# Block summaries of an attention kernel: sums of v by TensorE, maxima of k in token layout, query copies in a row, and a new order of steps

## Chip, core and metric

The program runs on one core of one Trainium2 chip. The metric is device time in microseconds (us) of one launch, on the slowest (here the only) core. Engines: TensorE (PE; PEld is its weight load), VectorE (DVE), ScalarE (ACT), GpSimd (POOL), SyncE (SP). Loads of q and k are issued by POOL (the software queue q0, which turns f32 into f16 on the way), all other transfers by SP (the hardware queue q1); 16 DMA engines serve both.

## The reference, cut to what matters

```python
# first part: q, k, v of shape (4, 8, 768, 64); blocks of 32 tokens, window 16
k_sum = k.reshape(B, H, nb, block, D).max(axis=3)       # 24 block maxima of k per head
v_sum = v.reshape(B, H, nb, block, D).mean(axis=3)      # 24 block means of v per head
scores_l = scale * q @ k.T                              # kept where |i - j| < 16
scores_s = scale * q @ k_sum.T + log(block)
a = softmax(concat[scores_l masked, scores_s])
x = a @ concat[v, v_sum]                                # heads side by side: (4, 768, 512)
# second part: 4 experts (Hd = 64), the best 2 of 4 by x @ w_gate with softmax weights w
for e in range(4):
    y = softmax_causal(scale * (x @ wq[e]) @ (x @ wk[e]).T) @ (x @ wv[e]) @ wo[e]
    out += w[e] * y
```

## The kernel before

There are four batches b. **Stage 1** is the first part of the reference, for a pair c of two heads at a time (c = 0 to 3, two pairs to a group g of four heads). A window of 96 keys and the 24 block maxima (120 rows) meet 64 queries in one score product; there are 12 such windows per head. The steps of a pair, in the names of the plan: `dk`, `dq` load k and q of a group as f16; `tk`, `tq` transpose them on TensorE; `ck`, `cq` copy the transposes from PSUM to kT and qT; `rk` takes the block maxima of kT (L305); `kw` and `ksc` put the windows and the maxima into kw; `sc` makes scores in two halves (mask by L361, product by L368), `ex` the exponentials aT, `av` the product with vb in f32 (L385, two halves), `rc` and `xm` divide, `tx` transposes back (L410), `hi` and `lo` split x into two f16 parts.

vb holds for each window its 96 rows of v and below them, in rows 96 to 119, the 24 block sums of the head, repeated for all 12 windows. The rows of v come by `dv` from memory (96 x 24 pieces of 256 B for a pair). The sums come in three steps: `dvs` loads v of a group a second time, with a block's 32 tokens side by side in one partition (tile vs, 768 KB); `tr` adds halves to halves, five additions on VectorE or POOL (L247); `ds` writes the result into vb by two transfers on SP's queue, which repeat each row 12 times (72 KB each).

**Stage 2** is the second part, for a batch: `pp` projects to queries and keys (L558), `vp` to values and gate logits (L493, L496), `ga` to `gc` compute the gate, `sp` scores (L582), `es` exponentials (L590), `dm` the causal mask on the diagonal (POOL, L595), `aw` the weighted values (L606), `r2`, `wv` weights them, `tw`, `ct` transposes, `op` projects out (L647), `oc` copies and `od` stores. The weights are loaded and cast once (`dw`, `dwv`, `dwo`, `cw`, `cvg`, `co`).

The order of all 734 steps, the engine of each, and the buffer that it takes are written in a table (L50 to L104); the program issues them as they stand there, and an engine and its queue keep that order. SLOTS gives the number of buffers of each kind. The qT copy `cq` writes, in even batches, with a step between elements, and in odd ones in a row:

```python
if b % 2:
    copy(e, dst.rearrange("c (p s) -> c p s", s=6), src.rearrange("c (s p) -> c p s", s=6))
else:
    copy(e, dst.rearrange("c (p s) -> c s p", s=6), src.rearrange("c (s p) -> c s p", s=6))
```

Of the kernel before, what the change touches and what calls it, by code (L numbers as in the profile page):

```python
# [50 lines left out]
19,S,0 4,G, 5,V, 20,V, 17,G,0 88,P,0.0 6,G, 21,V, 8,G, 22,V, 68,P,1.1 0,G,1 18,G,0 89,V, 91,A,0 73,P,0.0 3,G,1  # L51
69,V, 70,V,0 71,A,1 93,P,1.1 1,G, 72,A, 90,V,1 48,P,2.0 74,A, 94,A, 7,G, 77,P,4.0 78,A, 92,V, 23,G, 24,G,
95,P,0.1 75,P,6.2 76,A, 49,V, 51,V,2 50,V,1 52,V, 67,S,0 25,G,1 97,P,2.3 98,A, 66,S, 80,P,4.0.0 2,G, 53,P,6.2
54,V, 79,P, 28,P,2.1 9,S,1 81,V, 15,G, 96,A, 82,V, 33,P,3.0 29,V, 83,P,0.0.0 84,A, 57,P,4.4 58,A, 31,V,1
55,P,6.5 56,A, 213,G,2 283,P,2.0 30,V,0 32,A, 284,A, 87,S,2 86,S, 99,P,4.1.1 34,V, 35,P,2.0 36,A, 214,G,2
288,P,6.1 205,G,0 26,S, 10,G, 11,G, 85,V, 289,A, 37,P,0.2 12,G, 13,G, 14,G, 286,V,0 27,S, 100,P, 285,V,1
287,V, 101,V, 102,V, 223,P,2.1 224,V, 243,P,3.0 268,P,6.2 269,V, 292,P,4.1 38,A, 226,A,2 103,P,0.1.1 104,A,
244,V, 245,V,0 633,G,3 225,V,1 293,A, 227,V, 290,P,6.3 40,P,2.0.0 291,A, 105,V, 206,G,0 247,A,1 248,P,4.0
# [721 lines left out]
```

## Time and profile before

| what | us |
|---|---|
| median of 3 runs (lowest, highest) | 207.64 (206.0, 210.47) |
| the profiled execution's own time | 208.41 |
| its span on the chip | 206.4 |
| TensorE busy | 149.7 |
| VectorE busy | 131.6 |
| ScalarE busy | 123.1 |
| GpSimd busy | 82.8 |

The span runs from the first to the last recorded event of that execution; its own time is what was measured around it. Busy time is the sum in which an engine had an instruction at work; matmuls are pipelined, so a busy TensorE need not be at its peak. The DMA queues moved 33.17 MB in 65499 packets, 54208 of them under 512 B. A wait is put down to the event that ended it; `issue` is a wait for which the profile shows nothing.

### The profile page before, as it was taken

The page shows a single profiled execution, that of the slowest core. Times are in us where ns is not written, and L with a number is a line of the kernel's source. Part 1 is how long each engine was busy: PE and PEld are TensorE (multiplying, and loading weights), DVE is VectorE, ACT ScalarE, POOL GpSimd, SP SyncE. Part 2 cuts the span into 40 slices and gives each one's busy share as a digit, 9 for nine tenths or more (in the row PEclk, how much of TensorE's full clock was granted, in tenths as well). Part 3 has the DMA queues.
Part 4 walks back from the last instruction along what each step waited for, and adds up shares of the span by engine and source line. Part 5 has one row for each costly group of instructions (what it writes and reads, how often), then busy time and mean ns, then how long its engine had stood idle before and what let it go on. Part 6 is the DMA issues. An engine that isn't in the chain of part 4 may idle for free.

```text
span 206.4 us, 6279 instructions
## 1 busy us (share of the span) xinstructions
PE 149.7 (73%) x2704; PEld 115.2 (56%) x2704; DVE 131.6 (64%) x227; ACT 123.1 (60%) x152; POOL 82.8 (40%) x146
## 2 busy tenths in 40 slices
PE   0252277897369974737977978766999999999960
PEld 0242175686356753637754567655768767767620
DVE  0653029987666467604839998967498687636940
ACT  2199402658265854517997777344646888698740
POOL 7980009304520634236553954918722012223300
PEclk9999999999969999988999999999699999999997
DMA  6999999699999999999167997999698580200456
GB/s 154 187 150 187 223 175 148 80 183 208 167 199 230 168 163 183 204 210 246 24 105 128 219 184 113 219 260 265 105 175 166 139 137 17 89 3 0 165 194 254
DMA packets 65499, 33.17 MB, mean 161 GB/s; under 512 B 54208, under 2 KB 61376, under 8 KB 64704
## 3 DMA queue, kind: packets, MB, share of 16 engines
q1 hardware_dynamic: 58016, 26.48, 67.4%
q0 software_dynamic: 7456, 6.29, 20.2%
q8 instruction: 21, 0.34, 0.7%
q14 instruction: 6, 0.05, 0.1%
HBM read 30.41 MB, written 6.29 MB: 178 GB/s over the span
## 4 chain that ended last, share of the span: by engine, by line
PE 41%; DVE 21%; DMA 17%; issue 10%; ACT 6%; SPq 1%; POOL 1%; DVEq 0%; POOLq 0%; ACTq 0%
PE ps L385 9%; PE ps L558 7%; DMA vb<-in_v_dram 7%; DMA vb<-vs 7%; DVE qT L163 4%; PE ps L410 4%; PE ps L493 4%; PE ps L647 4%; PE ps L582 3%; DMA kn<-in_k_dram 3%; DVE ks L305 3%; PE ps L334 2%; PE ps L606 2%; PE ps L296 2%; DVE x L400 2%
## 5 line engine op out<-in xcount | busy, mean ns | idle before, releaser
L590 ACT ACTIVATE a<-ps 128x1024 f16<-128x1024 f32 (+1 forms) x48 | 42.0, 915 | 14.1 <-PE ps L582 12.6
L385 PE MATMUL ps<-vb,aT 120*64 120x65 f32 x768 | 30.1, 241 | 14.7 <-DMA vb<-in_v_dram 7.1
L595 POOL TENSOR_SCALAR_AFFINE_SELECT a<-a 128x256 f16<-128x256 f16 x48 | 18.9, 410 | 54.4 <-ACT a L590 49.6
L247 POOL TENSOR_TENSOR vs<-vs 96x1024 f32<-96x1024 f32 (+4 forms) x23 | 25.3, 1100 | 31.4 <-DMA vs<-in_v_dram 20.7
L385 PEld LDWEIGHTS ps<-vb,aT 120*64 120x64 f32 x768 | 27.8, 154 | 17.5 <-issue 11.9
L375 ACT ACTIVATE aT<-ps 120x768 f32<-120x768 f32 x32 | 25.2, 819 | 14.2 <-PE ps L368 11.3
L558 PE MATMUL ps<-hi,wqk 128*128 128x384 f16 x128 | 22.6, 326 | 1.6 <-ACT aT L375 1.6
L163 DVE COPY qT<-ps 128x768 f16<-128x768 f16 x6 | 12.9, 2145 | 12.4 <-PE ps L334 12.2
L163 POOL COPY kw<-kT 128x960 f16<-128x960 f16 (+1 forms) x14 | 15.7, 1153 | 11.6 <-PE ps L368 8.1
L410 PE MATMUL ps<-id,x 128*128 128x128 f32 x96 | 16.8, 320 | 4.5 <-issue 1.6
L421 DVE TENSOR_TENSOR lo<-ps,hi 128x768 f16<-128x768 f32 x16 | 15.4, 971 | 5.2 <-ACT hi L161 5.0
L361 PE MATMUL ps<-pi,mt 64*128 64x64 f16 (+1 forms) x128 | 12.8, 271 | 7.0 <-issue 3.3
L558 PEld LDWEIGHTS <-wqk 128*128 128x128 f16 x128 | 12.1, 98 | 9.4 <-issue 1.9
L296 PE MATMUL ps<-id,kn 96*64 96x96 f16 x256 | 10.1, 244 | 9.1 <-DMA kn<-in_k_dram 8.7
L410 PEld LDWEIGHTS ps<-id,x 128*128 128x128 f32 x96 | 12.7, 162 | 6.6 <-issue 2.1
L247 DVE TENSOR_TENSOR vs<-vs 96x512 f32<-96x512 f32 (+4 forms) x17 | 10.5, 615 | 8.9 <-DMA vs<-in_v_dram 7.0
L582 PE MATMUL ps<-qk,qk 64*128 64x512 f16 (+3 forms) x128 | 14.6, 307 | 2.1 <-DVE x L400 1.2
L368 PE MATMUL ps<-qT,kw 64*128 64x64 f16 x384 | 12.8, 204 | 4.2 <-ACT qT L161 2.3
L400 DVE TENSOR_TENSOR x<-ps,rec 128x768 f32<-128x768 f32 x16 | 15.3, 957 | 0.6
L161 ACT COPY qT<-ps 128x768 f16<-128x768 f16 x10 | 15.6, 1612 | 0.1
L161 ACT CAST hi<-ps 128x768 f16<-128x768 f32 x9 | 7.4, 825 | 13.5 <-PE ps L410 13.4
L305 DVE TENSOR_REDUCE ks<-kT 128x24 f16<-128x768 f16 x16 | 14.9, 944 | 0.1
(81 smaller groups left out, 260.8 us busy)
## 6 DMA issues: line engine op xcount, KB each, us to landing
vb<-in_v_dram SPq DMA_DIRECT2D x14, 576.0 KB
vs<-in_v_dram SPq DMA_DIRECT2D x8, 768.0 KB
out_dram<-ob SPq DMA_DIRECT2D x12, 512.0 KB
kn<-in_k_dram POOLq DMA_DIRECT2D x7, 384.0 KB, 6.9
qn<-in_q_dram POOLq DMA_DIRECT2D x7, 384.0 KB, 7.6
vb<-vs SPq DMA_DIRECT2D x32, 72.0 KB
vb<-in_v_dram SPq DMA_DIRECT2D x2, 552.0 KB
a<-in_moe_wq_dram SPq DMA_DIRECT2D x4, 128.0 KB
```

The costliest lines, as they stand in the source:

```text
L161: nc.scalar.copy(dst, src)
L163: en(e).tensor_copy(dst, src)
L247: en(e).tensor_tensor(w[:, 0:half], w[:, 0:half], w[:, half:2 * half], AL.add)
L305: nc.vector.tensor_reduce(T["ks"][ks.slot], T["kT"][kT.slot].rearrange("c (s n p) -> c n s p", s=8, n=NSUM), AX.XY, AL.max)
L375: nc.scalar.activation(T["aT"][aT.slot][0:KR], pbank(sc, 2)[0:KR, :, 0:384], AF.Exp, scale=SCALE)
L385: nc.tensor.matmul(pbank(av, 2)[o:o + 64, u, 65 * (2 * (t // 2) + hp):65 * (2 * (t // 2) + hp) + 65], a[0:KR, hp, 64 * t:64 * t + 64], T[" ...
L400: nc.vector.tensor_tensor(T["x32"][x32.slot].rearrange("p (u t w) -> p u t w", u=2, w=64), avv()[:, :, :, 0:64], T["rec"][rec.slot].to_bro ...
L410: nc.tensor.transpose(pbank(xp, 2)[:, t // 3, 128 * (t % 3):128 * (t % 3) + 128], T["x32"][x32.slot][:, 128 * t:128 * t + 128], T["id32"])
L558: nc.tensor.matmul(pbank(pp, 2)[:, u, 0:384], T["wqk"][:, ch, cc, j, :], hi_(ch)[:, 384 * u:384 * u + 384], start=(ch == 0), stop=(ch == N ...
L582: nc.tensor.matmul(pbank(sp, 2)[:, ep, c0:c0 + w], T["qk"][qk[1].slot][r, 128 * tj:128 * tj + 128], T["qk"][qk[0].slot][r, n0:n0 + w], sta ...
L590: nc.scalar.activation(a2v(u), pbank(sp, 2)[:, :, 0:ln], AF.Exp, scale=SCALE / (XS * XS))
L595: nc.gpsimd.affine_select(m, m, [[0, 2], [1, 128]], AL.is_ge, 0.0, base=0, channel_multiplier=-1)
```

## The change

Four things, and a new table.

- Block sums of v: `dvs`, `tr` and the transfers of `ds` go. TensorE sums the 96-row windows that `dv` has loaded: 12 products per head with a slice of a 0/1 matrix `sel` (made once on POOL) accumulate into 24 rows of PSUM (`bs`, L294, f32, 32 weight columns). Four heads lie in four groups of 32 PSUM partitions in batches 1 to 3, two in batch 0. `be` copies the sums to vs, partitions 96 to 119; `ds` is now a copy on POOL, VectorE or ScalarE that repeats them into vb.
- Maxima of k: `km` takes, on the loaded k (token layout, 8 tokens of a partition side by side), maxima of halves in three steps; two more transposes in `tk` bring the result to PSUM, and `rk` reduces only 4 to 1 there.
- q is loaded as 96 x 512 like k, and `cq` always writes qT in a row (its source in PSUM is read with a step).
- The weights are declared in parts (two halves of wqk, values, output), so that a projection waits only for its own.
- The table is new: the steps stand in another order, on partly other engines. vb has six buffers and ks three. The constants in braces in the step calls are the planner's estimates; they do not enter the program.

Core of the diff:

```diff
-SLOTS = dict(qn=3, kn=3, kT=2, ks=2, kw=3, qT=3, aT=6, x32=2, vb=4, vs=2,
+SLOTS = dict(qn=3, kn=3, km=3, kT=2, ks=3, kw=3, qT=3, aT=6, x32=2, vb=6, vs=2,
...
-19,S,0 4,G, 5,V, 20,V, 17,G,0 88,P,0.0 6,G, 21,V, 8,G, 22,V, 68,P,1.1 0,G,1 18,G,0 89,V, 91,A,0 73,P,0.0 3,G,1
+116,S,0 27,G,0 28,G,0 29,V,0 30,V, 31,V, 10,G, 76,P,0.0.0 12,V, 5,G,1 77,A, 94,P,1.1.1 99,P,2.0 78,V, 80,V,0
...
+    def sels(e):
+        z = T["sel"]
+        en(e).memset(z, 0.0)
+        nc.gpsimd.memset(z[:, 22:24], 1.0)
+        nc.gpsimd.affine_select(z[:, 22:24], z[:, 22:24], [[-32, 2]], AL.is_ge, 0.0,
+                                base=-16, channel_multiplier=1)
+        nc.gpsimd.affine_select(z[:, 22:24], z[:, 22:24], [[32, 2]], AL.is_ge, 0.0,
+                                base=47, channel_multiplier=-1)
...
+            for w in (256, 128, 64):
+                def mx(e, w=w, i=i):
+                    hs = slice(n * i, n * i + n)
+                    m = T["km"][km[b, g].slot][:, hs, :]
+                    x = T["kn"][kn[b, g].slot][:, hs, :] if w == 256 else m
+                    en(e).tensor_tensor(m[:, :, 0:w], x[:, :, 0:w], x[:, :, w:2 * w], AL.max)
...
-            nc.sync.dma_start(out=T["vs"][t.slot],
-                              in_=v[b, 4 * g:4 * g + 4].rearrange("h (n s) d -> (h n) (s d)", s=32))
-        R.step(f"dvs{b}{g}", {"S": 0.45}, [], [t], go, dma=2.2)
-        half = 1024
-        while half >= 64:
-            def add(e, half=half):
-                w = T["vs"][t.slot]
-                en(e).tensor_tensor(w[:, 0:half], w[:, 0:half], w[:, half:2 * half], AL.add)
...
-            for hp in range(2):
-                r0 = NSUM * (hh + hp)
-                nc.sync.dma_start(out=w[WIN:KR, 12 * hp:12 * hp + 12, 0:64],
-                                  in_=s[r0:r0 + NSUM, 0:64].unsqueeze(1).to_broadcast((NSUM, NQ, 64)))
...
+    def sums(b, cs):
+        sp, t = R.buf("ps"), R.buf("vs")
+
+        def mm(e):
+            n = 2 * len(cs)
+            for tt in range(NQ):
+                for j in range(n):
+                    nc.tensor.matmul(pbank(sp)[32 * j:32 * j + 32, 0, 0:64],
+                                     T["sel"][:, 22 - 2 * tt:54 - 2 * tt],
+                                     T["vb"][vb[b, cs[j // 2]].slot][0:WIN, 12 * (j % 2) + tt, 0:64],
+                                     start=(tt == 0), stop=(tt == NQ - 1))
...
+        def ev(e):
+            for j in range(2 * len(cs)):
+                copy(e, T["vs"][t.slot][96:120, j, :], pbank(sp)[32 * j:32 * j + NSUM, 0, 0:64])
...
+            def dsum(e, i=i, c=c):
+                copy(e, T["vb"][vb[b, c].slot][WIN:KR, :, 0:64].rearrange("n (h t) d -> n h t d", h=2),
+                     T["vs"][t.slot][WIN:KR, 2 * i:2 * i + 2, :].unsqueeze(2).to_broadcast(
+                         (NSUM, 2, NQ, 64)))
...
+            for hp in range(2):
+                nc.tensor.transpose(pbank16(kp)[64 * hp:64 * hp + 64, 768:864],
+                                    T["km"][km[b, g].slot][:, hh + hp, 0:64], T["id16"][0:96, 0:96])
...
-                                    T["kT"][kT.slot].rearrange("c (s n p) -> c n s p", s=8, n=NSUM),
-                                    AX.XY, AL.max)
+                                    pbank16(kp)[:, 768:864].rearrange("c (n p) -> c n p", p=4),
+                                    AX.X, AL.max)
...
-            if b % 2:
-                copy(e, dst.rearrange("c (p s) -> c p s", s=6),
-                     src.rearrange("c (s p) -> c p s", s=6))
-            else:
-                copy(e, dst.rearrange("c (p s) -> c s p", s=6),
-                     src.rearrange("c (s p) -> c s p", s=6))
+            copy(e, T["qT"][qT.slot].rearrange("c (p s) -> c p s", s=8),
+                 pbank16(qp)[:, 0:S].rearrange("c (s p) -> c p s", s=8))
...
+            for c in (2 * g, 2 * g + 1):
+                load_v(b, c)
+                if b == 0:
+                    sums(b, [c])
+            if b:
+                sums(b, [2 * g, 2 * g + 1])
```

What the new table does to the order, at three places. First SyncE's queue at the start of the program, before (vs are the tiles of the tree, vb those of the products; the number behind a name tells buffers apart):

```order
L240 DMA vs_100<-in_v_dram 96x2048
L286 DMA vb_96<-vs_100 24x12x64 x2
L268 DMA vb_96<-in_v_dram 96x24x64
L240 DMA vs_101<-in_v_dram 96x2048
L286 DMA vb_98<-vs_100 24x12x64 x2
L268 DMA vb_98<-in_v_dram 96x24x64
L262 DMA vb_97<-in_v_dram 80x64
L268 DMA vb_97<-in_v_dram 96x23x64
```

and after (L466, L472 and L459 are loads of weights into buffers named a and wg):

```order
L466 DMA a_136<-in_moe_wq_dram 128x4x64
L275 DMA vb_101<-in_v_dram 80x64
L281 DMA vb_101<-in_v_dram 96x23x64
L281 DMA vb_102<-in_v_dram 96x24x64
L281 DMA vb_103<-in_v_dram 96x24x64
L281 DMA vb_104<-in_v_dram 96x24x64
L466 DMA a_136<-in_moe_wk_dram 128x4x64 x2
L472 DMA a_137<-in_moe_wv_dram 128x4x64
```

The loads of vb stood behind loads of vs and behind transfers that wait for sums; now the four of batch 0 stand together behind one load of weights.

Second GpSimd at the start, before (its first instructions behind the constants; kn and qn are k and q as loaded, id an identity, kw and vb are given their constant parts):

```order
L181 AFFINE_SELECT id_63<-id_63 128x128
L227 DMA kn_75<-in_k_dram 96x4x512
L209 MEMSET kw_82 128x12x8
L210 MEMSET kw_82 128x16
L211 MEMSET kw_82 128x16
```

and after:

```order
L241 DMA kn_79<-in_k_dram 96x4x512
L241 DMA qn_72<-in_q_dram 96x4x512
L184 MEMSET id_63 128x128
L185 ISA
L185 AFFINE_SELECT id_63<-id_63 128x128
L241 DMA kn_80<-in_k_dram 96x2x512 x2
L208 MEMSET vb_101 128x24
```

Loads of k and q moved to the front of the engine; eleven more memsets of vb, two of v2, two loads of q and the memset of vb's first rows (`zv00`) follow, and the first load of vb waits for the last of these.

Third TensorE at the first `av` of the program, before (L368 ends the scores, L385 is `av`, L334 transposes queries):

```order
L368 LDWEIGHTS kw_82
L368 MATMUL ps<-qT_86,kw_82 128x64
L368 LDWEIGHTS kw_82
L368 MATMUL ps<-qT_86,kw_82 128x64
L385 MATMUL ps<-vb_96,aT_88 64x65 x12
L334 LDWEIGHTS qn_73
L334 MATMUL ps<-id_63,qn_73 64x128
```

and after (L391 the scores, L294 the block sums, L408 `av`, L321 transposes keys):

```order
L391 LDWEIGHTS kw_89
L391 MATMUL ps<-qT_91,kw_89 128x64
L294 MATMUL ps<-vb_102,sel 32x64 x24
L408 MATMUL ps<-vb_101,aT_97 64x65 x12
L408 MATMUL ps<-vb_101,aT_98 64x65 x12
L408 MATMUL ps<-vb_102,aT_94 64x65 x12
L408 MATMUL ps<-vb_102,aT_93 64x65 x12
L321 LDWEIGHTS kn_81
```

A block sum of 24 products now stands ahead of the first `av`, and four `av` steps follow one another.

## Rows read from the trace of the kernel before

**Rows 1.** Windows by stage: length; busy PE, PEld, DVE, ACT, POOL; PEclk, DMA share, GB/s.

```profile
0.00:61.62 61.62, 32.37 (x665) 28.17 (x666) 35.40 (x49) 30.34 (x34) 25.85 (x58) 0.97 1.06 172
61.62:99.63 38.01, 28.26 (x506) 22.20 (x506) 19.84 (x45) 21.29 (x27) 14.76 (x22) 0.96 1.19 195
99.63:150.59 50.96, 40.82 (x804) 30.86 (x801) 40.20 (x61) 34.72 (x45) 31.94 (x40) 0.97 0.91 165
150.59:176.12 25.53, 25.35 (x452) 19.18 (x451) 20.61 (x41) 18.41 (x26) 4.34 (x12) 1.00 0.66 131
...
sum 206.40, PE 149.69 PEld 115.22 DVE 131.62 ACT 123.13 POOL 82.80; mean PE 29.94 PEld 23.04 DVE 26.32 ACT 24.63 POOL 16.56
```

**Rows 2.** The chain that ended last, its shares of the span by line.

```profile
by line: issue 10.3%; PE ps L385 8.9%; PE ps L558 7.1%; DMA vb<-in_v_dram 6.8%; DMA vb<-vs 6.6%; DVE qT L163 4.1%; PE ps L410 4.1%; PE ps L493 3.7%; PE ps L647 3.6%; PE ps L582 3.4%; DMA kn<-in_k_dram 3.2%; DVE ks L305 2.5%; PE ps L334 2.1%
```

**Rows 3.** Waits of TensorE over the span: total us, times, longest us.

```profile
PE ps L385 <- DMA vb<-in_v_dram: 7.1, 2, 5.6
PE ps L385 <- DMA vb<-vs: 6.9, 3, 4.2
PE ps L361 <- issue: 3.3, 1, 3.3
...
PE ps L334 <- DVE qT L163: 1.5, 1, 1.5
...
PE ps L410 <- ACT qT L161: 1.1, 1, 1.1
```

**Rows 4.** SyncE's timeline (start us, us, what): the first load of vb.

```profile
13.12 0.54 SPq L268 DMA_DIRECT2D vb<-in_v_dram  x1
```

**Rows 5.** Groups of instructions by shape, whole span: busy us, mean ns of one.

```profile
L227 POOL DMA_DIRECT2D kn<-in_k_dram x9 | 6.3, 697 | 0.2 <-issue 0.2
...
L396 DVE RECIPROCAL rec<-ps 128x12 f32<-128x12 f32 x16 | 3.8, 234 | 14.3 <-PE ps L385 14.2
...
L247 DVE TENSOR_TENSOR vs<-vs 96x1024 f32<-96x1024 f32 x2 | 2.4, 1222 | 7.0 <-DMA vs<-in_v_dram 7.0
```

**Rows 6.** DMA packets, 48 to 58 us; software queue (packets, MB, share), 0 to 61.62 us.

```profile
DMA packets 5482, 1.89 MB, mean 189 GB/s; under 512 B 5402, under 2 KB 5402, under 8 KB 5402
...
q0 software_dynamic: 3744, 3.15, 34.2%
```

**Rows 7.** TensorE's timeline: start us, us, line, operation, shape, count, wait before.

```profile
27.28 1.57 PE L385 MATMUL ps<-vb,aT 120*64 120x65 f32 x24 [5.57 <-DMA vb<-in_v_dram]
...
67.93 0.33 PE L361 MATMUL ps<-pi,mt 64*128 64x320 f16 x4
68.09 0.34 PE L368 MATMUL ps<-qT,kw 64*128 64x64 f16 x12
68.27 0.33 PE L361 MATMUL ps<-pi,mt 64*128 64x64 f16 x4
...
90.91 2.87 PE L385 MATMUL ps<-vb,aT 120*64 120x65 f32 x48 [4.22 <-DMA vb<-vs]
...
129.26 0.53 PE L296 MATMUL ps<-id,kn 96*64 96x96 f16 x16
...
129.96 1.57 PE L385 MATMUL ps<-vb,aT 120*64 120x65 f32 x48
```

**Rows 8.** Instructions on tile qT: ns min/median/max, first and last start.

```profile
L161 ACT COPY qT<-ps x10: 798/835/2921, 14.3 to 165.9; 128x768 f16<-128x768 f16 x10
L163 DVE COPY qT<-ps x6: 942/2726/2775, 29.6 to 130.2; 128x768 f16<-128x768 f16 x6
```

**Rows 9.** Page, groups of instructions: busy us, mean ns of one.

```profile
L247 DVE TENSOR_TENSOR vs<-vs 96x512 f32<-96x512 f32 (+4 forms) x17 | 10.5, 615 | 8.9 <-DMA vs<-in_v_dram 7.0
...
L305 DVE TENSOR_REDUCE ks<-kT 128x24 f16<-128x768 f16 x16 | 14.9, 944 | 0.1
```

**Rows 10.** Windows of TensorE alone: busy us (records), PEclk, DMA share, GB/s.

```profile
0.00:52.80 52.80, 28.23 (x605) 1.00 1.07 170
...
0.00:137.00 137.00, 90.76 (x1753) 0.98 1.05 173
```

More of the change, by code (lines that the diff above doesn't have):

```diff
@@ L470, in cw @@
                 s = slice(1024 * i, 1024 * i + 1024)
-                copy(e, T["wqk"].rearrange("p c a j n -> p (c a j n)")[:, s], f32(sA)[:, s])
-            R.step(f"cw{i}", {"V": 1.1, "G": 1.4, "A": 1.0}, [sA], [wqk], cw)
+                copy(e, T["wqk"].rearrange("p a c j n -> p (a c j n)")[:, s], f32(sA)[:, s])
+            R.step(f"cw{i}", {"V": 0.68, "G": 1.04, "A": 1.0}, [pw[i]], [wqk[i]], cw, keep=[sA])
         def co(e):
             copy(e, T["wo"].rearrange("p c n -> p (c n)"), f32(sB)[:, 1024:2048])
-        R.step("co", {"V": 1.1, "G": 1.4, "A": 1.0}, [sB], [wo], co)
+        R.step("co", {"V": 0.68, "G": 1.04, "A": 1.0}, [po], [wo], co, keep=[sB])
     def stage2(b, hs, ls):
@@ L545, in gc @@
             w.tensor_tensor(g4(5), g4(4), bc(g1(1)), AL.mult)
-        R.step(f"gc{b}", {"V": 0.9}, [gt], [gt], gc)
+        R.step(f"gc{b}", {"V": 0.84}, [gt], [gt], gc)
         wTs = []
@@ L660, in stage2, with fill @@
             R.step(f"od{b}{t2}", {"S": 0.45}, [ob], [], od, dma=256 * 0.09 / 16)
+    def fill(bank, n):
+        for _ in range(n):
+            nc.tensor.matmul(T["ps"][:, bank, 0:128], T["id16"], T["id16"], start=True, stop=True)
+    R.fill = fill
     load_qk(0, 0, 2)
-    R.step("id16", {"G": 0.5}, [], [id16], lambda e: ident(T["id16"], 128)(e))
-    R.step("pi", {"V": 0.5}, [id16], [pi], pis)
-    R.step("kwz", {"V": 0.6, "G": 0.9}, [], [kwpad], kwz)
-    R.step("mt", {"G": 1.6}, [], [mt], masks)
-    R.step("vone", {"V": 0.9, "G": 0.9}, [], [vones], vone)
-    load_vs(0, 0)
-    R.step("id32", {"G": 0.5}, [], [id32], lambda e: ident(T["id32"], 128)(e))
-    R.step("v2o", {"V": 0.3, "G": 0.4}, [], [v2one], v2o)
-    hl = []
+    R.step("id16", {"G": 0.6}, [], [id16], lambda e: ident(T["id16"], 128)(e))
+    R.step("pi", {"V": 0.52}, [id16], [pi], pis)
+    R.step("kwz", {"V": 0.6, "G": 0.72}, [], [kwpad], kwz)
+    R.step("mt", {"G": 3.0}, [], [mt], masks)
+    R.step("vone", {"V": 0.9, "G": 1.5}, [], [vones], vone)
+    R.step("sel", {"G": 1.0}, [], [sel], sels)
+    R.step("id32", {"G": 0.6}, [], [id32], lambda e: ident(T["id32"], 128)(e))
+    R.step("v2o", {"V": 0.3, "G": 0.31}, [], [v2one], v2o)
     for b in range(B):
@@ L689, in decode @@
         i, e, s = w.split(",")
-        out.append((int(i), e, [int(x) for x in s.split(".") if x]))
+        out.append((int(i) if i != "f" else -1, e, [int(x) for x in s.split(".") if x]))
     return out
@@ L717 @@
     one("pi", (128, 6, 64), HALF)
-    one("wqk", (128, NCH, 2, 2, 128), HALF)
+    one("wqk", (128, 2, NCH, 2, 128), HALF)
     one("wvg", (128, NCH, 264), HALF)
@@ L722 @@
     one("wgt", (128, NCH, 4), FP32)
-    many("qn", (128, 4, 384), HALF)
+    many("qn", (96, 4, 512), HALF)
+    many("km", (96, 4, 256), HALF)
+    one("sel", (96, 54), FP32)
     many("kn", (96, 4, 512), HALF)
```

255 lines of the change are left out of this document (129 added, 126 removed).

## Prediction, made blind from the rows above

> **What bounds the kernel now.** I cut the span at the first projections `pp` of batches 0, 1, 2 and 3 (L558 in TensorE's timeline, starts at 61.6, 99.6, 150.6 and 176.1 us) and asked the table of windows for each stretch [rows 1]. Look at TensorE and DMA in each row. In the head (0 to 61.6) TensorE is busy 32.4 us and DMA's share is 1.06: the queues are full (over 1 means that packets overlap in the count). From 61.6 to 99.6 the share is 1.19 and TensorE is busy 28.3 of 38.0 us; from 99.6 to 150.6 it is 40.8 of 51.0; from 150.6 to 176.1 it is 25.35 of 25.53, and there TensorE alone is the bound. The last 30.3 us (206.4 - 176.1) are batch 3's second stage and the last stores. Over the whole span no engine is near its limit (TensorE 149.7, VectorE 131.6, ScalarE 123.1), so the question is what TensorE waits for.
>
> The chain that ended last gives it by line [rows 2]: transfers into vb take 6.8% (from v) and 6.6% (from vs), 27.7 us together, the qT copies of VectorE 4.1%, `issue` 10.3%. TensorE's own waits [rows 3] say what was really lost: 7.1 us on vb from v, 5.6 of it one wait, in the head; 6.9 us on vb from vs, 4.2 of it one; 1.5 and 1.1 us on qT copies (smaller ones left out); and stops put down to nothing, the longest 3.3 us. SyncE's queue shows why the head is long [rows 4]: the first load of vb from v is issued only at 13.1 us, because the spread `ds` of another pair, which must wait for the tree of additions, stands ahead of it in a strict queue.
>
> **The change, part by part.** The sum is made on the profiled execution: span 206.4 us, its own time 208.4, so 2.0 us lie around the span. That time is 0.4% above the median of the three runs shown.
>
> *Head.* Two loads of vs and batch 0's eight spread transfers are gone, and SP's waits for the tree. After, SP issues one weight load and then all four vb loads of batch 0; the first of them needs POOL's `vone` and `zv00`, which stand behind six issues of k and q loads and some twenty small instructions. An issue takes POOL 0.70 us [rows 5], so 4.2; with the preamble's 0.8 and an estimated 0.15 for each small one this is about 8.5 us, where it was 13.1. From then on transfers set the pace. Price: 5482 packets, nearly all under 512 B, went through in 10 us of full queues [rows 6], 548 per us. The four vb loads are 9216 packets of 256 B: 16.8 us. Twelve loads of wq, wk and wv are 6144: 11.2 us. In the old head the software queue's 3744 packets took 34.2% of 16 engines in 61.62 us [rows 6], 0.090 us each; batch 0's k and q (1536 packets) are so 8.6 us on 16 engines, batch 1's two early loads 4.3. Together 40.9, plus 1 of start: 42. If packets overlapped as in the second stretch (share 1.19), 36.
> TensorE is a second bound there. Until about 43 us it ran at half its later speed: 24 records of L385 take 1.57 us at 27.3, and 48 take 1.57 at 130 [rows 7], though the granted clock reads 1.00 there. Its 32.4 us of head work lose 4.2 (moved work, below, at this speed) and gain four block sums of 3.2: 41 us from about 7 on, so 48 if the speed never rose. In the old head it rose in an unbroken run of matmuls, and a backlog makes such a run. I take **43**, with 36 and 50 as ends: 18.6 us saved.
>
> *Block sums.* Ten steps `bs`: 48 fp32 products each for batches 1 to 3 (six steps), 24 for batch 0 (four). L385's 12 products show as 24 records, so these are 96 and 48 records. No row has products with 32 weight columns. Lower bound: L368 starts 12 records at 68.09, and the next line starts at 68.27 [rows 7], 15 ns each, so 96 take 1.4 us. Upper bound: L385 takes 33 ns per record with two column halves at work, 66 in one half; with no overlap 96 take 6.3 us. Four column groups at 66 ns give 16 ns and 1.5 us. Since the halves do overlap in L385, I take 1.5 (and 1.6 for a small step with two groups, twice that at half speed). Behind the head that is 6 x 1.5 = **+9.0**.
> The Trainium skill, page "TensorEngine Tiling (Array Packing)", section "Performance Considerations", speaks against it: a matmul has about 60 cycles of overhead, so one with a single column takes as long as one with 60. That would be 25 ns at 2.4 GHz, 2.4 us per step, 5.4 us more in all. L368's 15 ns do not agree with it.
>
> *Moved work.* Before, the transposes of all four pairs of batch 1 and the scores of three stand ahead of the first projection; after, those of two pairs. Two key and two query steps (0.35 each, L296 and L334 at 129.26 to 129.96) and two scores (0.34, L361 and L368 from 67.93 to 68.27 [rows 7]) move into the middle: **+2.1**. Two more key transposes for each of ten pairs there: +0.4.
>
> *Waits.* The spread transfers end, and with six vb buffers for four the loads of batch 1 are asked for before its scores need them, so 6.9 and 1.5 (7.1 - 5.6) us go: **-8.4**. Late next could be the copy `ds` on the chip; other steps of TensorE stand between its sum and its `av`. Query copies: the rows of qT [rows 8] read 0.80, 0.84 and 2.92 us (min, median, max) on ScalarE and 0.94, 2.73 and 2.78 on VectorE. The long ones are the eight of even batches, which write with a step of 12 bytes; the short ones write in a row, as all sixteen do after. That frees 8 x 1.8 = 14 us of engine time, and the waits of 1.5 and 1.1: **-2.6**. After the 4.2 us wait that ends at 90.9, L385 x48 took 2.87 us instead of 1.57 [rows 7]: **-1.3**.
>
> *VectorE.* It loses 10.5 us of the tree and 14.9 of key maxima (L305) [rows 9], and 7 with four strided copies. It gains the maxima `km`, eight groups of 1024, 512 and 256 elements. The nearest row is the f32 addition, 1.22 us for 1024 [rows 5], so 2.1 per group and 17; 16-bit operands could halve that, no row shows it. Sixteen small maxima and 26 evictions at 0.23 (L396 [rows 5]) are 10, seven spreads of 1536 elements at 1.8 are 13. So 131.6 - 32 + 40 = 139 us in a span of 187: covered by TensorE's 165, and thinly where both are dense.
>
> *Code.* The 3.3 us stop falls behind the 605th record of TensorE and another behind the 1753rd [rows 10], nine times 128 apart but for 4: it looks like the fetch of program text (128 matmuls and their weight loads) behind full queues. The new program crosses seven such borders more, and its queues are emptier: I count 0. If one crossing in five stops for 3.3 us, as now at most, it is 4.6, an end for the range. The Trainium skill, page "Runtime: NRT & Kernel Launch", section "Instruction fetch mechanics", has blocks of 256 instructions too, but calls the crossing mostly hidden; the 3.3 us row is not.
>
> **Sum.** Head 43. Middle (61.6 to 176.1, 114.5 us): +9.0 + 2.1 + 0.4 - 8.4 - 2.6 - 1.3 = 113.7. The last stretch has the same 38 steps of TensorE: 30.3. Together 187.0, with the 2.0 around it **189 us**.
>
> **Rivals.**
> *The middle tightens too.* Of the 20 us that TensorE idles in it (114.5 - 94.4 busy) 9 stay in my sum. If 5 more go and the head is 37, it is 178. For it: the third batch's stretch, with DMA at 0.66, has no idle. Against: VectorE and ScalarE carry much in the same stretches.
> *A longer head or slower sums.* The head at 50, or `bs` at L385's 33 ns per record (3.2 us each, +10): 196 to 199. The skill's 60 cycles lie inside this. For it: the half speed lasts 43 us now.
> *Nothing gained in the middle.* The waits come back as others, since VectorE or POOL (whose spreads hold its queue) becomes late: +12.3, and some for code: 203. Against: the waits that go are transfers, which no engine repeats.
> *Slower.* One mechanism: 32-column products do not overlap. At 66 ns per record 96 take 6.3 us: six steps +29, four of 3.2 instead of 1.6, at half speed, +6: 224. It is slower from +23 us, 212, on, with 768 records about 30 ns more on each. For it: no row shows this shape. Against: L385's halves overlap.
>
> **How the numbers follow.** Forecast 0.50 (182 to 194), tighter middle 0.15, long head or slow sums 0.18, nothing gained 0.10, no overlap 0.07. The range of 175 to 203 leaves out the last and half of the one before. Within 2% (203.5 to 211.8, about what a measurement can tell from no change) lies most of "nothing gained": 0.09. Slower 0.07, faster 0.84.
>
> **What would show it.** The first vb load issued near 8.5 us; the first projection (`pp`, whatever its new line) near 43; no wait of SP for an adder; TensorE waiting for vb under 2 us in the middle; 96 records of a block sum in 1.5 us; every qT copy under 1 us; a km group within 2.1 us. The prediction is wrong if the first projection starts after 50, if `bs` takes over 3 us, or if the middle takes more than 120.

## The result, and the profile after

The changed kernel takes 197.46 us (median of 4 runs, 196.76 to 197.92), the one before 207.94 beside it: ratio 0.952, 95% interval 0.944 to 0.960. The forecast was 189.0 in a range of 175 to 203. Ratios here and below leave disturbed runs out; medians don't. The profiled execution has a span of 196.1 us. By stage, in us (the predicted ends are the prediction's own):

| stretch | before [rows 1] | predicted | after |
|---|---|---|---|
| head, to the first `pp` | 61.6 | 43 | 43.3 |
| middle, to batch 3's first `pp` | 114.5 | 113.7 | 120.8 |
| last stretch | 30.3 | 30.3 | 32.0 |

So the head's time came out as forecast, and the middle got longer where a small gain was forecast. Windows by stage, columns as in [rows 1], for the changed kernel (`pp` is now L582):

```profile
0.00:43.30 43.30, 30.77 (x804) 27.63 (x805) 28.46 (x60) 20.30 (x31) 23.34 (x52) 1.00 1.11 176
43.30:81.23 37.93, 35.15 (x772) 27.55 (x773) 31.45 (x62) 25.38 (x34) 15.46 (x24) 0.96 1.08 166
81.23:140.81 59.58, 49.63 (x1215) 39.03 (x1214) 44.27 (x86) 34.07 (x47) 30.08 (x36) 0.94 0.60 107
140.81:164.12 23.31, 23.26 (x494) 18.18 (x492) 16.83 (x30) 16.57 (x22) 6.05 (x11) 1.00 0.13 48
164.12:196.08 31.96, 23.51 (x288) 14.83 (x286) 18.99 (x44) 16.77 (x22) 5.40 (x14) 0.94 0.27 100
```

The third row is the place: 59.6 us where the kernel before took 51.0, with TensorE busy 49.6, a DMA share of 0.60 (0.91 before) and a granted clock of 0.94. What TensorE waited for there is in its waits over the span (total us, times, longest), which answer to [rows 3]:

```profile
PE ps L321 <- DMA kn<-in_k_dram: 6.6, 1, 6.6
PE ps L294 <- issue: 4.7, 2, 4.3
PE ps L408 <- issue: 3.8, 3, 1.8
PE ps L362 <- ACT a L614: 1.8, 1, 1.8
```

No row has vb or qT any more: the waits of [rows 3] on transfers into vb and on query copies are gone. The largest after the first load are stops that the profile puts down to nothing. TensorE's timeline shows two of them, and block sums (L294) of 48 records in the head and of 96 behind it, at both speeds (start, us, wait before):

```profile
18.94 2.77 PE L294 MATMUL ps<-vb,sel 96*32 96x64 f32 x48
...
22.48 1.55 PE L294 MATMUL ps<-vb,sel 96*32 96x64 f32 x48
...
111.83 1.22 PE L294 MATMUL ps<-vb,sel 96*32 96x64 f32 x70
117.36 1.01 PE L294 MATMUL ps<-vb,sel 96*32 96x64 f32 x26 [4.31 <-issue]
...
119.69 2.28 PE L294 MATMUL ps<-vb,sel 96*32 96x64 f32 x96
...
124.64 0.88 PE L408 MATMUL ps<-vb,aT 120*64 120x65 f32 x24
127.16 1.22 PE L408 MATMUL ps<-vb,aT 120*64 120x65 f32 x24 [1.63 <-issue]
...
148.86 1.56 PE L294 MATMUL ps<-vb,sel 96*32 96x64 f32 x96
```

70 records go, then TensorE stands for 4.31 us in the middle of one block sum, and the profile shows no operand that it waits for. Behind the stop the same 96 records take 2.28 instead of 1.56 us: from 117.4 to 120.7 us the granted clock is 0.50, and then it rises again.

The other lines that answer to rows of before. SyncE's first load of v, at 13.12 in [rows 4]:

```profile
8.53 0.35 SPq L275 DMA_DIRECT2D vb<-in_v_dram  x1
```

The copies on tile qT (count, ns min/median/max), 2.7 to 2.9 us for the long ones in [rows 8]:

```profile
L165 ACT COPY qT<-ps x11: 799/804/823, 10.5 to 136.0; 128x768 f16<-128x768 f16 x11
L167 DVE COPY qT<-ps x5: 945/946/957, 37.6 to 149.3; 128x768 f16<-128x768 f16 x5
```

VectorE's new groups (busy us, mean ns), where [rows 9] had the tree and the old maxima:

```profile
L251 DVE TENSOR_TENSOR km<-kn 96x1024 f16<-96x1024 f16 x7 | 6.5, 923 | 6.7 <-DMA kn<-in_k_dram 6.6
...
L167 DVE COPY vs<-ps 24x64 f32<-24x64 f32 x26 | 5.8, 222 | 9.0 <-PE ps L294 8.6
...
L251 DVE TENSOR_TENSOR km<-km 96x512 f16<-96x512 f16 x7 | 4.3, 620 | 0.2
...
L251 DVE TENSOR_TENSOR km<-km 96x256 f16<-96x256 f16 x9 | 2.5, 283 | 0.2
```

### The profile page after: what moved, and what is told of

It is laid out like the page before. It is cut to its first block, busy times and chain, and to the rows that moved or that the text cites. A ratio compares the mean times of both kernels' runs of the same rounds, so it can differ in the third digit from the quotient of the medians.

```text
span 196.1 us, 7990 instructions
## 1 busy us (share of the span) xinstructions
PE 162.3 (83%) x3568; PEld 127.2 (65%) x3568; DVE 140.0 (71%) x279; ACT 113.1 (58%) x152; POOL 80.3 (41%) x137
## 4 chain that ended last, share of the span: by engine, by line
PE 66%; DVE 19%; issue 7%; ACT 3%; DMA 3%; DVEq 0%; ACTq 0%; POOLq 0%
PE ps L408 13%; PE ps L582 8%; PE ps L294 7%; PE ps L630 6%; PE ps L433 5%; DVE kw L167 5%; PE ps L671 5%; PE ps L517 4%; PE ps L606 4%; PE ps L384 4%; DVE km L251 3%; PE ps L321 3%; PE ps L391 3%; DMA kn<-in_k_dram 3%; PE ps L362 2%
## 5 line engine op out<-in xcount | busy, mean ns | idle before, releaser
L614 ACT ACTIVATE a<-ps 128x1024 f16<-128x1024 f32 (+1 forms) x48 | 41.9, 918 | 6.5 <-PE ps L606 5.9
L167 POOL COPY kw<-kT 128x960 f16<-128x960 f16 (+1 forms) x20 | 24.5, 1256 | 25.6 <-ACT kT L165 23.4
L408 PE MATMUL ps<-vb,aT 120*64 120x65 f32 x768 | 28.3, 230 | 5.0 <-issue 3.8
L408 PEld LDWEIGHTS ps<-vb,aT 120*64 120x64 f32 x768 | 25.5, 143 | 7.8 <-issue 5.6
L582 PE MATMUL ps<-hi,wqk 128*128 128x384 f16 x128 | 22.5, 326 | 0.0
L294 PE MATMUL ps<-vb,sel 96*32 96x64 f32 x768 | 18.4, 233 | 4.7 <-issue 4.7
L294 PEld LDWEIGHTS ps<-vb,sel 96*32 96x32 f32 x768 | 16.2, 118 | 6.6 <-issue 6.2
L167 POOL COPY vb<-vs 24x1536 f32<-24x1536 f32 x8 | 12.9, 1611 | 14.5 <-DVE vs L167 12.2
L582 PEld LDWEIGHTS <-wqk 128*128 128x128 f16 x128 | 12.0, 98 | 8.2 <-issue 0.5
L321 PE MATMUL ps<-id,kn 96*64 96x96 f16 x256 | 9.9, 230 | 8.6 <-DMA kn<-in_k_dram 6.6
L165 ACT COPY kT<-ps 128x768 f16<-128x768 f16 x8 | 6.4, 801 | 15.2 <-PE ps L324 11.8
L321 PEld LDWEIGHTS <-kn 96*64 96x64 f16 x256 | 8.3, 128 | 9.8 <-DMA kn<-in_k_dram 6.6
L517 PE MATMUL ps<-wvg,hi 128*128 128x264 f16 x96 | 13.8, 275 | 0.0
L433 PE MATMUL ps<-id,x 128*128 128x128 f32 x96 | 13.3, 278 | 0.1
L671 PE MATMUL ps<-wo,wT 128*128 128x512 f16 x48 | 12.7, 397 | 0.6 <-ACT a L614 0.3
L391 PE MATMUL ps<-qT,kw 64*128 64x64 f16 x384 | 12.5, 201 | 0.0
## 6 DMA issues: line engine op xcount, KB each, us to landing
vb<-in_v_dram SPq DMA_DIRECT2D x14, 576.0 KB, 10.2
```

What stands on the lines that cost most here:

```text
L167: en(e).tensor_copy(dst, src)
L294: nc.tensor.matmul(pbank(sp)[32 * j:32 * j + 32, 0, 0:64], T["sel"][:, 22 - 2 * tt:54 - 2 * tt], T["vb"][vb[b, cs[j // 2]].slot][0:WIN, 12 ...
L321: nc.tensor.transpose(pbank16(kp)[64 * hp:64 * hp + 64, 96 * s:96 * s + 96], src[:, hh + hp, 64 * s:64 * s + 64], T["id16"][0:96, 0:96])
L408: nc.tensor.matmul(pbank(av, 2)[o:o + 64, u, 65 * (2 * (t // 2) + hp):65 * (2 * (t // 2) + hp) + 65], a[0:KR, hp, 64 * t:64 * t + 64], T[" ...
L433: nc.tensor.transpose(pbank(xp, 2)[:, t // 3, 128 * (t % 3):128 * (t % 3) + 128], T["x32"][x32.slot][:, 128 * t:128 * t + 128], T["id32"])
L517: nc.tensor.matmul(p[:, i, 0:264], hi_(ch)[:, cols], T["wvg"][:, ch, :], start=(ch == 0), stop=False, skip_group_check=True)
```

## The experiments

Runs stand in sets with their own runs of the kernel before (e1 to e4, e5 to e8, e9 to e11, e12). Medians in us, ratio to the kernel before of the set where there is one, span of the profiled run and its first `pp`:

| run | what | median (lowest, highest) | ratio [95%] | span | first `pp` |
|---|---|---|---|---|---|
| e5 | changed kernel again | 199.79 (197.24, 201.08) | 0.966 [0.950, 0.982] | 195.5 | 44.3 |
| e1 | qT by steps, batches 0, 2 | 208.81 (207.02, 211.18) | 1.014 [0.998, 1.029] | 209.3 | 52.4 |
| e11 | qT by steps, batch 0 | 208.15 (201.5, 210.21) | none | 205.5 | 56.6 |
| e6 | before, qT in a row | 205.12 (201.71, 207.49) | 0.983 [0.964, 1.002] | 205.5 | 61.0 |
| e7 | first load of v later | 202.89 (199.94, 204.95) | 0.973 [0.956, 0.991] | 203.2 | 47.8 |
| e2 | sums of 1 product | 189.21 (185.67, 193.16) | none | 184.0 | 41.9 |
| e3 | no maxima in batches 1 to 3 | 200.03 (195.92, 202.72) | none | 198.2 | 45.0 |
| e4 | no v loads, batches 2, 3 | 190.64 (188.64, 190.72) | 0.931 [0.920, 0.942] | 188.9 | 42.9 |
| e8 | v loads early | 195.71 (193.06, 196.79) | 0.943 [0.922, 0.965] | 194.0 | 44.0 |
| e9 | and a sum apart | 194.29 (192.47, 194.91) | 0.938 [0.931, 0.946] | 192.0 | 42.8 |
| e10 | and a q load early | 192.51 (192.18, 194.85) | 0.934 [0.926, 0.942] | 193.1 | 43.3 |
| e12 | 64 small products more | 199.35 (196.33, 202.23) | 0.963 [0.953, 0.972] | 194.6 | 43.9 |

The measure beside e6 to e8 is the changed kernel again:

> The changed kernel itself, as measure for its neighbours in this set: 197.5 us, first projection at 43.

Its profile has stops put down to nothing behind the same records of TensorE (350, 1496, 1752, 2135 and 2262; not behind 478 and 2518, where the first profile has them too). It has more half speed in the long stretch (granted 0.88 for 0.94), which takes 58.1 us.

### What made the head short

**e7, the first load of v later.** On POOL, step 18 (`zv00`) moves behind step 13 (the masks):

```diff
...
-18,G,0 13,G,
+13,G, 18,G,0
...
```

> One step moved: the memset zv00, for which the first load of v waits, stands behind the masks on POOL; the first load of v comes some 3 us later, at 11.5. If transfers set the head from there on, as the prediction has it, the first projection moves by the same 3 us to 46.3, and the time to 200.5. If TensorE's or ScalarE's work sets the head, it stays near 43.5: 197.5 to 198.

SyncE's first load of v, TensorE's longest wait in the head behind the first load of k, and the head's window:

```profile
11.94 0.35 SPq L275 DMA_DIRECT2D vb<-in_v_dram  x1
```

```profile
PE ps L294 <- DMA vb<-in_v_dram: 3.7, 1, 3.7
```

```profile
0.00:47.77 47.77, 33.46 (x805) 29.79 (x805) 28.89 (x60) 20.18 (x31) 23.37 (x52) 0.93 1.08 169
```

The load comes 3.4 us later and the first `pp` 3.5 later than in e5 of the same set (4.5 later than in the changed kernel's first profile). Of these 3.5 us, 1.5 are the new wait for v (3.7) less a stop of 2.2 that e5 has there and e7 has not; 2.0 are TensorE's own work, 33.5 us for 31.4, at a granted clock of 0.93 for 0.96. By time alone the two don't part: the ratios are 0.973 and 0.966, and their intervals overlap.

So a load of v that comes 3.4 us later holds TensorE. That the head of the changed kernel runs at the pace of the queues is not shown by this, and the profile speaks against it. These are TensorE's waits in that head:

```profile
PE ps L321 <- DMA kn<-in_k_dram: 6.6, 1, 6.6
PE ps L408 <- issue: 1.8, 1, 1.8
PE ps L324 <- DVE km L251: 1.7, 2, 1.0
PE ps L384 <- DVE pi L202: 1.4, 1, 1.4
```

Behind the first load of k TensorE waits for no transfer; in the 36.7 us from there to the first `pp` it is busy for 30.8. With v early, TensorE's own work sets this head. In the kernel before, 5.6 us of waits on v and 5.1 on qT copies stood between its steps.

**e6, the kernel before with query copies in a row.**

```diff
...
-            if b % 2:
+            if True:
...
```

> The kernel before with one part of the change alone: the query copies of even batches write in a row, as those of odd ones do; order, loads and sums are the old ones. By the prediction's step (waits of 1.5 and 1.1 us in the middle) it gives 2.6 us: 205. Theory copies (what undoing this part cost the changed kernel, some 10 us, nearly all in the head, is what the part is worth anywhere): 198, with the first projection at 53 or earlier instead of 61.6. Theory order (the old head is set by the first load of v at 13 us and by full queues, behind which the long copies hide): first projection at 60 to 62, and 204 to 206.

```profile
0.00:61.02 61.02, 28.53 (x664) 24.76 (x665) 32.10 (x49) 26.31 (x34) 26.56 (x58) 0.96 1.01 166
```

TensorE's longest wait in that head:

```profile
PE ps L385 <- DMA vb<-in_v_dram: 10.7, 1, 10.7
```

The head stays at 61.0 (61.6 before). Of the 5.1 us of waits on qT in it 0.6 are left, and the wait for v grew from 5.6 [rows 3] to 10.7: theory order. The ratio of 0.983 would be 3.5 us, but its interval reaches 1: what this part is worth alone, in the old order, is not clear of noise.

**e1 and e11, the same part undone in the new order** (e11 with `if b:`, so in batch 0 alone):

```diff
-            copy(e, T["qT"][qT.slot].rearrange("c (p s) -> c p s", s=8),
-                 pbank16(qp)[:, 0:S].rearrange("c (s p) -> c p s", s=8))
+            dst, src = T["qT"][qT.slot], pbank16(qp)[:, 0:S]
+            if b % 2:
+                copy(e, dst.rearrange("c (p s) -> c p s", s=8),
+                     src.rearrange("c (s p) -> c p s", s=8))
+            else:
+                copy(e, dst.rearrange("c (p s) -> c s p", s=8),
+                     src.rearrange("c (s p) -> c s p", s=8))
```

> The changed kernel (197.5 us) with one part undone: the query copies of batches 0 and 2 write with a step again. The copies on qT should rise from at most 0.95 to some 2.7 us in eight pairs, 14 us of engine time. By the prediction's step (waits of 1.5 and 1.1 us that go) the undoing costs 2.6 us: 200.1. If those waits were only taken over by others, it costs nothing: 197.5. If VectorE is what holds the middle, its three longer copies there cost 5 us: 202.5.

> The changed kernel with the query copies of batch 0 alone writing with a step (four copies, all on ScalarE in the head). Theory copies in the head (with the loads of v early, ScalarE's long copies are next to hold TensorE there): first projection at 50 to 53 instead of 43 to 44, and the time some 8 us above the changed kernel, 205 to 208. If the head of e1 was late for something else, or if TensorE catches up later: 198 to 200.

Head of e1, then its copies on qT (ns min/median/max):

```profile
0.00:52.42 52.42, 33.37 (x805) 29.00 (x806) 28.60 (x60) 30.97 (x31) 22.98 (x52) 0.90 1.15 177
```

```profile
L165 ACT COPY qT<-ps x11: 800/3587/3909, 10.6 to 149.2; 128x768 f16<-128x768 f16 x11
L167 DVE COPY qT<-ps x5: 947/958/3601, 45.2 to 162.5; 128x768 f16<-128x768 f16 x5
```

All three numbers of e1's expectation were too small: the head alone grew by 9.1 us (52.4), ScalarE's work in it from 20.3 to 31.0, and the whole gain of the change was gone. Of the 9.1 us, 5.0 are TensorE's waits on ScalarE's copies to qT, which the changed kernel's head doesn't have, and 2.6 are its own work at a granted clock of 0.90. In e11, with batch 0 alone, these waits are 5.7 us and the first `pp` stands at 56.6 (one wait on the split of x, 4.4 us, comes on top); three of its runs take 207 to 210 us, but one takes 201.5, so how much of e1's loss batch 0 makes is open. One caution: q now lies 8 tokens to a partition, so the step is 16 bytes and not 12, and a copy takes up to 3.9 us where [rows 8] had 2.7 to 2.9. Four copies in the head are thus some 4 us dearer than the old ones would be, so the old step would have cost less than the 9; how much was not run.

Both together: with v late, long copies hide behind the wait for v (e6); with v early, they hold TensorE themselves (e1). In these runs neither part gives the 18 us of the head without the other.

### Is it the work of the block sums, or VectorE?

**e2, sums of one product per head.**

```diff
...
-            for tt in range(NQ):
+            for tt in range(1):
...
```

> The block sums with one product per head instead of twelve (eleven windows of each head's sums are left out): 704 of 3568 records of TensorE go, everything else stays. Theory code: the middle is late because the instructions of 128 records come later than short records use them up, and because the clock falls after such stops; then the six large sums give back 6 x 1.4 = 8.5 us of work behind the head, and most of the 7.6 us of stops put down to nothing and some 3 us of half-speed with them: 179 to 182. Theory work: only the work goes: 189. Theory VectorE: TensorE waits for VectorE instead: 192 or more. In all of them the first projection stays near 43 us if transfers set the head.

```profile
0.00:41.85 41.85, 28.24 (x629) 24.74 (x630) 28.97 (x60) 20.20 (x31) 23.25 (x52) 0.96 1.10 171
76.88:128.92 52.04, 46.17 (x951) 35.79 (x950) 44.13 (x86) 34.07 (x47) 30.85 (x36) 0.90 0.71 124
```

The head barely moves (41.9): its sums lose 2.5 us of TensorE's work, and a wait of 1.3 us for v comes in. The profile's span fell by 12.1 us, 7.5 of them in the stretch that was long. The four runs spread from 185.7 to 193.2; the two lower ones, 185.7 and 186.9, lie between theory code (179 to 182) and theory work (189), so the time doesn't separate them. The stops do say something: with the loads of v as they were, those put down to nothing are 3.2 us in the two long stretches, where the changed kernel has 7.6. The short records have a part in them.

**e3, no maxima in batches 1 to 3** (one memset at the start gives the third km tile a value).

```diff
...
+                    if b:
+                        return
...
```

> The maxima km of batches 1 to 3 are left out (18 instructions of VectorE, 6 x 1.83 = 11 us; the rest of the key maxima then works on old values). Theory VectorE (it is what holds the middle): 11 us less of it give 5 us or more, 192.5 or less. Theory code: at most the waits of TensorE for ks and vs go, 2 us: 195.5 to 197.5, with the stops put down to nothing as before.

```profile
85.91:143.66 57.75, 49.30 (x1216) 38.84 (x1214) 36.25 (x74) 33.74 (x47) 28.75 (x36) 0.94 0.62 111
```

VectorE has 8 us less in this stretch (36.3 for 44.3), the stretch is 1.8 shorter, and even the lowest run, 195.9, stays above the 192.5 of theory VectorE, which falls.

### The stops, and the clock behind them

**e4, no loads of v in batches 2 and 3.**

```diff
...
+            if b > 1:
+                return
...
```

> The loads of v of batches 2 and 3 are left out (8 x 2304 packets; the products then work on v of earlier batches). TensorE waits for no load of v in the middle of the changed kernel, so waits on data can't shrink. Theory code, with the fetch queued behind data packets: the 4.3 us stop near 113 falls to about 1.5, and the half-speed stretch behind it goes: 193. Theory code without queues: the stops stay as they are, 197. If the queues play no part at all: 197.5.

The long stretch, then TensorE in it (the block sum is L296 here):

```profile
80.77:133.56 52.79, 46.23 (x1215) 36.65 (x1214) 44.39 (x86) 34.18 (x47) 31.17 (x36) 1.00 0.28 66
```

```profile
110.30 1.22 PE L296 MATMUL ps<-vb,sel 96*32 96x64 f32 x71
112.27 0.56 PE L296 MATMUL ps<-vb,sel 96*32 96x64 f32 x25 [0.74 <-issue]
...
121.48 0.86 PE L410 MATMUL ps<-vb,aT 120*64 120x65 f32 x22 [1.58 <-issue]
```

No instruction of any engine waits for these loads in the changed kernel's profile, and yet leaving them out makes the stretch 6.8 us shorter: the 4.31 us stop is 0.74, all stops of the stretch fall from 7.2 to 3.3, and TensorE's busy time for the same 1215 records from 49.63 to 46.23, at a granted clock of 1.00. The stop of 1.6 us stays. The gain was larger than theory code with queues gave (190.6, not 193). It is not the luck of one profile: behind record 2262 the stop is 2.6 to 4.6 us in all seven profiles of the changed order whose loads and sums stand as here (the changed kernel, e1, e3, e5, e7, e11, e12), and at most 2.0 in the four that leave loads out or move them (e4, e8, e9, e10).

What comes late is on a queue of its own. The changed kernel's page has 28 packets of 16 KB on queue q8 `instruction`, the one before 21; TensorE has 7136 and 5408 records (matmuls and weight loads), that is one packet for each 256 of them (about 255 and 258), 128 matmuls. For the 4.31 us stop (113.05 to 117.36) I asked the queues of two windows, 109.8 to 114.3 and 114.3 to 115.8:

```profile
q1 hardware_dynamic: 1815, 0.64, 72.0%
q0 software_dynamic: 400, 0.39, 51.9%
q14 instruction: 1, 0.01, 0.4%
```

```profile
q1 hardware_dynamic: 813, 0.20, 87.8%
q8 instruction: 1, 0.02, 5.6%
```

The border before had been passed at 109.8. For 4.5 us no packet of q8 came while 2216 others went through; then it came, and 1.6 us after 115.8 TensorE went on. All seven stops of the changed kernel end 1.3 to 1.6 us after a packet of q8 has landed.

**e12, the borders moved.** The table's entry for filling, `f`, stands behind the first transposes, with 16 columns instead of 128:

```diff
...
+f,P,7.64
...
```

> The changed kernel with 64 small products of the identity (16 columns) added on TensorE behind its first transposes; nothing else moves. In the changed kernel the stops put down to nothing stand behind records 350, 478, 1496, 1752, 2135, 2262 and 2518, each 86 to 94 past a multiple of 128. Theory code: they come at the same counts of the new numbering (so at other instructions, 64 records earlier in the program), and none stays with its old instruction (new counts 414, 2199, 2326, 2582). If something in the data or the buffers makes them, they stay with their instructions. The time: no theory wants a gain; blocks with two sums in them fall otherwise, so 195 to 201.

TensorE alone, windows that end inside a stop: length, busy us (records). The changed kernel, then e12:

```profile
0.00:25.50 25.50, 15.18 (x350) 1.00 1.14 176
...
0.00:115.00 115.00, 93.73 (x2262) 0.99 1.01 163
```

```profile
0.00:21.50 21.50, 13.14 (x350) 1.00 1.13 172
0.00:27.50 27.50, 17.43 (x478) 1.00 1.17 176
...
0.00:71.00 71.00, 54.89 (x1368) 0.98 1.14 174
0.00:97.00 97.00, 78.17 (x1879) 0.98 1.08 164
0.00:115.00 115.00, 93.66 (x2262) 0.99 1.00 157
```

The counts are the same, 350, 478 and 2262, and others that are as far past a multiple of 128; the instructions are others, 64 records earlier. None stays at 414, 2199, 2326 or 2582. Over the fourteen profiles, 73 of the 75 stops put down to nothing stand 86 to 95 records past a multiple of 128; the other two are one stop of 1.5 us behind record 200, in the heads of e1 and e11. With e4 this shows that the stops belong to the program's text in blocks of 128 products, and that data packets make them longer.

The Trainium skill, page "Runtime: NRT & Kernel Launch", section "Instruction fetch mechanics", has the blocks of 256 instructions, fetched ahead by the engine's sequencer over a DMA queue, and calls the crossing mostly hidden. The blocks agree with the 28 packets; hidden it is not, with 7.2 us of stops in the 59.6 us stretch.

**e8, e9, e10: against the stops.** e8: a seventh vb buffer, and the last two loads of v right behind `dv31`, in an idle stretch of the queues.

```diff
...
-565,S,1
+565,S,1 575,S,6 577,S,
...
```

> A seventh buffer for vb, and the last two loads of v issued right behind dv31 (at 84 us), so that none is under way at 107 to 117 us but dv23. Theory code with queues (the fetch of program text waits behind data packets, and blocks of short records are used up sooner than the next one comes): the 4.3 us stop near 113 shrinks to 1.5 or less and the clock does not fall behind it, 5 to 7 us: 191 to 193. The price is more packets from 84 to 101, with two borders in them: up to 2 us back. If the stops have nothing to do with the queues: 197.5.

e9 moves a block sum (steps 566, 567) from just ahead of another to the wide products of stage 2, 46 steps earlier; e10 moves on POOL the load of q (step 223) ahead of a mask (step 156).

> e8 (a seventh vb buffer, the last loads of v early) with one step more moved on TensorE: the block sum bs30 stands some 260 records earlier, among the wide products of stage 2, and no longer just ahead of bs22. Theory code: 128 records with a block sum among them are used up in 2.5 to 3.3 us, sooner than the next 128 come; with the two sums apart the stop before the second one (0.9 us in e8) and the 1.5 us one ahead of them go below 0.5, and with them one stretch of half speed: 2 to 4 us less than e8, 192 to 194. If the stops depend on the queues alone: as e8, 195 to 196.

> e9 with the load of q of the second half of batch 1 moved on POOL ahead of a mask that waits 11 us for an exponential (issued at 38.6 instead of 50.2 us). TensorE's 1.8 us wait at 56 us and the half-speed stretch behind it (1.7 us) should go: 3 us less than e9. Against it: in the head, which transfers set, its packets (about 4 us of all queues) now come before the first projection, which could move from 44 to 46: then no gain, or 1 us.

The long stretch in e8, e9 and e10:

```profile
81.99:138.86 56.87, 51.02 (x1215) 40.15 (x1214) 43.18 (x86) 34.00 (x47) 30.07 (x36) 0.91 0.62 113
```

```profile
82.07:136.86 54.79, 46.81 (x1215) 36.91 (x1214) 45.42 (x86) 34.00 (x47) 30.79 (x36) 1.00 0.66 117
```

```profile
83.89:138.01 54.12, 47.66 (x1215) 37.73 (x1214) 44.85 (x86) 34.07 (x47) 30.70 (x36) 0.97 0.66 120
```

e8 lost the stop behind record 2262; its median is 4.1 us below e5's where 5 to 7 were expected, but the intervals of the two ratios overlap. Its stretch is only 1.2 us shorter, since stops of 1.5 and 1.9 us and three stretches at half speed remained. In e9 the stop before the second sum fell to 0.3, but 2.0 us came back at record 2262, now at another line; no half speed in the stretch. In e10 the wait at 56 us is gone, but the block sum behind it now stops for 1.8 us with half speed after it, and batch 0's second stage (40.6 us) is no shorter; its interval overlaps e9's, as e9's does e8's: the single steps are not apart. Ratios of 0.938 and 0.934 against 0.952 and 0.966 of the changed kernel: e10, at 192.5 us, beats both kernels beyond the intervals, with all of the work still in it. Two of its three parts treat the text's lateness; what the third, the load of q, gives by itself is not shown.

## Why the prediction was right, and where it was off

The change was forecast at 19 us, and 10.5 came; the time lies in the range. By one of the prediction's own signs it fails: the middle takes 120.8 us, and 120 was the limit (119.3 in e5, 118.8 in e12).

**Head: the time right (43, measured 43.3), the bound not the one named.** The first load of v was issued at 8.53 (8.5 predicted). "From then on transfers set the pace" did not come true: behind the first load of k TensorE waits for none. The second bound set the head. The prediction put 41 us of TensorE's work behind the first 7, were its speed not to rise, and said that a backlog would raise it. It rose at 21.8 us instead of 43, in a run without a wait since 16.0: 48 records of a block sum take 2.77 us at 18.9 and 1.55 at 22.5. The four sums so took 7.4 us and not 12.8, and the whole work 30.8. That this ends near the sum of transfers (42) is in part luck: v is not far behind (in e2, with less work in the head, TensorE waits 1.3 us for it), but nothing waits for the weights.

One link was missing: the working took the query copies as a matter of the middle alone. With its "smaller ones left out" it misread TensorE's waits: the profile of before has 2.3 and 2.0 us on ScalarE's qT copies, in the head, more than the 1.5 and 1.1 counted. e1 shows that with strided writes the first `pp` would have stood behind 43, though its step is dearer than the old one.

**Block sums: the size right, one argument wrong.** 96 records take 1.56 to 1.57 us at the upper speed (1.5 predicted), and the 48 of a small step 1.54 to 1.55 (1.6): four column groups take twice the records in the time of two. Products with 32 weight columns overlap, and the slower rivals fall. But "66 in one half", which prices the upper bound and the rival "slower", is the row at 27.3 of [rows 7], which the head's own paragraph puts down to half speed. At the upper speed one half of L385 takes 0.92 us, 38 ns a record:

```profile
46.37 0.92 PE L385 MATMUL ps<-vb,aT 120*64 120x65 f32 x24
```

Against the 33 ns of two halves that shows next to no overlap in L385, so the sums' overlap did not follow from it. The Trainium skill, page "TensorEngine Tiling (Array Packing)", section "Performance Considerations", has about 60 cycles for a matmul; at 2.4 GHz that would be 25 ns, an estimate. The trace has 16 ns a record.

**VectorE: the total by luck.** It is 140.0 us busy (139 predicted), and no bound (e3). But the new groups take 32.4 us where the sum had 40 (km 14.8 of 17, spreads 7.9 of 13; a km group 1.83 us, evictions 222 ns). What fills the gap was not in the sum: the new table gives VectorE more of other copies (those to kw rose from 11.3 to 16.9 us, to ob from 6.1 to 9.7, to qk from 2.9 to 6.7).

**Waits: right, on transfers and on copies.** No wait on vb, none on qT. The middle's idle time fell from 20.1 to 12.8 us, where -8.4 and -2.6 wanted 9.1.

**Code: the step that failed.** "The new program crosses seven such borders more, and its queues are emptier: I count 0." In the two long stretches before, stops put down to nothing are 4.3 us (1.9, 1.6 and 0.8); after, 7.6. That is the missing 3.7 us of idle time but for 0.4. The number of borders was the wrong measure: block sums put 96 of a block's 128 products into 1.5 us, so a block is used up before the next one is there (e2, e12), and loads of v in flight delay that one (e4).

**Half speed: the other term.** TensorE's busy time in the middle was to grow by 11.5 us of work less 1.3 of slow clock that ends; it grew by 13.6 (94.4 to 108.0). In e4, with one slow stretch in the middle instead of three, it is 104.5: the work is as predicted (94.4 + 10.2), and 3.5 us are clock. The 1.3 us that the end of one long wait was to give back went to the stops that came in its place. Together 3.3 and 3.4 of the middle's 7.1 us.

**Last stretch: +1.7 us, not tested by a run.** In the profile its last two result copies stand on VectorE one behind the other (2.4 us, where one on each engine ended it before); the rest is waits of 1.0 us and less.

The rival "nothing gained in the middle" is the one that came nearest, and in its way: new waits took the place of some that were removed, but at the borders of the program's text and not, as it had it, on VectorE or POOL. Its +12.3 stands above the forecast's middle of 113.7; measured are +7.1.

## What to carry to other kernels

When products become many and short, look at how long TensorE takes for 128 of them, not only at their sum: where the program's text comes by DMA, stops of up to 4 us fell at fixed counts here, and transfers that no instruction waits for made them longer. A term whose number comes out may still rest on the wrong bound: ask the new profile which engine waits there. And a cost that is hidden in one order can hold the next one: price a copy against the wait that covers it, and again with that wait gone.

## What was not expected of the hardware

- A 16 KB packet of program text for every 128 products of TensorE; a stop at the border ends 1.3 to 1.6 us after the packet has landed. With few data packets in flight stops are 0.7 to 1.6 us (e4's long stretch), with 2216 in 4.5 us one is 4.3. The packets before the 1.6 us stops of e4 and of the changed kernel start as a load of q ends. In queues empty but for it (e4, from the border passed at 112.3 to the one at 115.7 us) the packet starts 1.1 us after the border, takes 0.9, and TensorE goes on 1.4 later; 128 products that were used up sooner than those 3.4 us stopped there for 1.0. Why the packet is not under way earlier stays open.
- The clock behind a stop: after stops of 4.3 and 1.6 us the granted clock was 0.50, the lower level of 1.2 GHz (117.4 to 120.7 us for the first); in e9 it did not fall after 2.0 and 1.4. It fell after a wait on another engine too (the 1.8 us that end at 58.2; 0.50 from 59.3 to 62.7).
- Copies from PSUM that write f16 by steps: 2.7 to 2.9 us at 12 bytes, 3.6 to 3.9 at 16, 0.80 to 0.96 in a row.
